# Weight conversion in three places of a step, one raw reload, eight transfers of v for a pair

## Chip, cores and metric

The kernel runs on one core of a Trainium2 chip. The metric is device time in microseconds (us), from the start to the end of one execution. Three runs of the kernel before took 1021.04, 1021.47 and 1020.66 us (median 1021.04).

## What is computed

Attention over the 256 channels of q, k and v (N = 6016 rows), and behind it two dense layers with a hidden width of 2048, all in float32:

```
qn = q / (norm(q, axis=rows) + 1e-6);  kn = k / (norm(k, axis=rows) + 1e-6)
s  = kn.T @ qn / tau;  s = s - s.max(-1);  a = exp(s);  a = a / (a.sum(-1) + 1e-9)
x  = v @ a                                        # 6016 x 256
x  = (h * sigmoid(1.702 * h)) @ w_out,   h = x @ w_in      # layer one
x  = max(0.01 * h, h) @ w2_out,          h = x @ w2_in     # layer two
```

The four weight matrices come as float64 numbers, seen by the kernel as pairs of 32-bit words.

## The kernel before

**Tiling.** The 6016 rows are cut into 6 pairs of two blocks of 512 rows (448 in the last pair). Each layer treats the pairs one after another: `steps` lists 12 of them, numbered i = 0 to 11, layer one being i = 0 to 5. Within a pair there are 8 steps f = 0 to 7; step f takes two blocks of 128 hidden units, f and f + 8. Every float32 operand is split into a high and a low part (`halves`, `subtract`), and every product is three matmuls (`terms`, L94).

**Four forms of a step.** Pair 0 is done plainly (`hidden_first`, L894), while the attention matrix is folded into `w_in` (`fold`, L685). Pairs 1 to 3 use `step` (L995): the hidden products come from seven block products on seven sums of weight blocks (A11, A12, A22, S1 to S4), the output products are plain: 45 matmuls a step. From pair 4 on (`FIRST`) `strassen_step` (L1082) does the output products in seven block products too: 39 matmuls a step, and weights are streamed from DRAM (`stream_in`, `stream_out`). The last two steps are plain again.

**Work on the weights.** For each f there are four pieces: `wi`, `wo` (layer one) and `w2i`, `w2o` (layer two). `convert` (L215) makes float32 of the two words: a scaling on ScalarE (`scale_words`, L192), three bit operations on VectorE (L225, L230, L234), then the high part as a cast and the low part as a subtraction. `combine` (L181) makes the sums of blocks with four additions of 128x128. The pieces of layer one are written raw to DRAM (`w1raw`, `o1raw`), and read back later one by one into `ts` (`load_first`, L311) for `combine_first` and `combine_out`, which also cast and subtract on VectorE. Results for streaming go to DRAM tiles `w1a`, `w1o`, `w2a`, `w2o`, with high parts first and low parts behind them.

**Order.** The whole order is written by hand: engines get their instructions in the order of the Python statements. The work on the weights is one generator (`jobs`, L348). `go_on(n)` takes n pieces from it, `to_mark` goes on to the next mark. In `step`, one `to_mark` stands ahead of the step's last output products (L1042) and one at its end (L1056); behind each stands `fetch` (one move of the next pair's input: a transpose from `xr` to `stg`, a subtraction, or a cast with a subtraction; `prefetch`, L785). In the next step VectorE then makes the low part of `gd` (`finish_step`, L1048, called by `next_stage` at L1013), and adds `tt` (L1020). TensorE's product S4 (L1033) writes to `pa`, which that addition reads, so it waits for it; after S4 VectorE adds `cc` (L1034). On ScalarE the copy to `tt` (L1016) is followed by the cast of `g11` (L1025), the activation of `tt`, the cast of `g22` (L1028) and the activations of `cc`.

**Buffers.** `xr` has two buffers of 512 columns, filled by four transfers each (`load`, L792), so 16 a pair. `cv` (raw words) has three, `ta` two and `ws` (cast parts) two buffers. All these transfers are issued by SP's queue.

Of the kernel before, what the change touches and what calls it, by code (L numbers as in the profile page):

```python
# [7 lines left out]
F32 = mybir.dt.float32  # L8
# [9 lines left out]
def tile_kernel(  # L18
# [31 lines left out]
    P = 128  # L50
# [69 lines left out]
    with tc.manual_schedule():  # L120
# [5 lines left out]
        def weights(pool, f):  # L126
            wa[f] = pool.tile([P, 2, 7, P], F32R, tag=f"wa{f}", name=f"wa{f}")
            wo[f] = pool.tile([P, 2, 2, C], F32R, tag=f"wo{f}", name=f"wo{f}")
# [48 lines left out]
        def next_load():  # L177
            if to_load and len(raws) < 3:
                load_piece(to_load.pop(0))

# [34 lines left out]
        def convert(key):  # L215


            name, f = key
            if key not in scaled:
                scale_words(raws[key])  # L220
                scaled.add(key)
# [17 lines left out]
            next_load()  # L239
            scale_next()  # L240
            yield
            a = a.bitcast(F32)
            flat = a.rearrange("p k c -> p (k c)")
            if name == "wo":
                hi, lo = (wo[f][:, s].rearrange("p k c -> p (k c)") for s in range(2))
                for j in range(2):
                    nc.sync.dma_start(
                        out=o1raw[f][:, 0::3] if j == 0 else o1raw[f][:, 1:3],
                        in_=a[:, 2 * j:2 * j + 2],
                    )  # L250
# [5 lines left out]
            if name == "wi":  # L256
# [14 lines left out]
            yield name == "w2i"  # L271
            if name == "w2o":
                if f >= REST:
                    nc.vector.tensor_copy(hi[:, 7], a[:, 3])
                    yield
                    subtract(lo[:, 7], a[:, 3], hi[:, 7].bitcast(F32))
                    yield
                raw = early.tile([P, P], F32, tag="wr", name="wr")
                nc.vector.tensor_copy(raw, a[:, 1])
                nc.sync.dma_start(out=w2r[:, f], in_=raw)  # L280
                yield True
            yield from combine(a)
            nc.vector.tensor_copy(hi[:, 3:7], a)
            yield
            def keep_block(x, n):
                if name == "w2i":
                    nc.sync.dma_start(out=w2a[f][:, n], in_=x[:, :7].bitcast(F32))
                elif f >= REST:
                    nc.sync.dma_start(out=w2o[f][:, n], in_=x.bitcast(F32))
                else:  # L290
                    for at in (slice(0, 3, 2), slice(3, 7)):
                        nc.sync.dma_start(out=w2o[f][:, n, at], in_=x[:, at].bitcast(F32))

            keep_block(hi, 0)
# [1164 lines left out]
```

## Time and profile before

| what | value |
|---|---|
| median of three runs | 1021.04 us |
| the profiled execution's own time | 1019.2 us |
| its span, first to last instruction | 1017.3 us |
| TensorE (PE) busy, share of the span | 1006.0 us, 99% |
| VectorE (DVE) busy | 894.2 us, 88% |
| ScalarE (ACT) busy | 727.8 us, 72% |
| chain that ended last | PE 88%, DVE 6%, DMA 3%, issue 2%, ACT 1% |

The profile is of one execution, and shorter than the median of the timed runs by 1.8 us. A busy PE is not a PE at its peak, since matmuls overlap and their ends are modelled: so the table does not tell how much time is lost in a stretch, and starts of matmuls have to be compared. The steps of pairs 1 to 3 lie between 147 and 397 us of the span, the first step with streamed weights begins at 396.73 us. The rows themselves stand two sections further down.

### The profile page before, as it was taken

To read this page: it belongs to the slowest core of one execution; us is meant where nothing else is said; L and a number is where in the kernel's file an instruction comes from. 1 tells how busy PE (TensorE), PEld (TensorE's weight loads), DVE (VectorE), ACT (ScalarE), POOL (GpSimd) and SP (SyncE) were. 2 spreads that over 40 slices of the span, in tenths; PEclk is the share of its full clock that TensorE was granted. 3 is DMA by queue.
4 is the path that set the end of the run, shared out by engine and by line. 5 is a ranking of instruction groups with operands and counts; after the bars stand their busy time and mean duration, and the time that the engine had idled before them with its cause. 6 is when DMAs were issued, how large, how long until landed. Compare 5 with 4: busy or idle time off the path is not lost.

```text
span 1017.3 us, 13086 instructions
## 1 busy us (share of the span) xinstructions
PE 1006.0 (99%) x4416; PEld 817.5 (80%) x4416; DVE 894.2 (88%) x1331; ACT 727.8 (72%) x1139; POOL 0.8 (0%) x7
## 2 busy tenths in 40 slices
PE   9999999999999999999999999999999999999998
PEld 7888877778788887787897887887887787787896
DVE  7899877888998998898998998998998998998985
ACT  7675456667677666787786886886887787687682
POOL 0000000000000000000000000000000000000000
PEclk9999999999999999999999999999999999999999
DMA  9866557655535854675766755865866765765662
GB/s 349 261 172 200 156 192 209 222 174 160 181 113 164 243 198 142 192 243 166 263 220 197 255 191 171 231 211 178 227 194 201 186 228 182 199 231 169 174 206 45
DMA packets 187186, 200.88 MB, mean 197 GB/s; under 512 B 102128, under 2 KB 144624, under 8 KB 185968
## 3 DMA queue, kind: packets, MB, share of 16 engines
q1 hardware_dynamic: 182832, 199.07, 62.9%
q10 hardware_dynamic: 4288, 0.98, 0.5%
q8 instruction: 35, 0.57, 0.2%
q14 instruction: 31, 0.25, 0.1%
HBM read 155.19 MB, written 44.83 MB: 197 GB/s over the span
## 4 chain that ended last, share of the span: by engine, by line
PE 88%; DVE 6%; DMA 3%; issue 2%; ACT 1%; SPq 1%; DVEq 0%; ACTq 0%
PE h L98 49%; PE y L98 16%; PE y L739 13%; PE y L1190 5%; PE y L465 4%; DMA qk<-in_k_dram 1%; DVE ta L234 1%; DVE ta L230 1%; DMA cv<-in_moe_w_in_dram 1%; DVE gd L105 1%; DMA ts<-w1raw 0%; DVE gd L102 0%; DVE ta L105 0%; DVE tt L105 0%; DVE ta L225 0%
## 5 line engine op out<-in xcount | busy, mean ns | idle before, releaser
L98 PE MATMUL h<-xa,wi 128*128 128x512 f32 (+1 forms) x765 | 200.9, 384 | 0.0
L98 PE MATMUL y<-g,wo 128*128 128x512 f32 (+1 forms) x744 | 198.4, 388 | 0.5 <-issue 0.5
L98 PEld LDWEIGHTS h<-xa,wi 128*128 128x128 f32 x765 | 142.9, 188 | 27.3 <-ACT tv L1098 1.4
L98 PEld LDWEIGHTS y<-g,wo 128*128 128x128 f32 x744 | 139.1, 188 | 29.7 <-issue 4.5
L98 PE MATMUL h<-xb,wi 128*128 128x512 f32 (+1 forms) x573 | 152.8, 391 | 0.1
L105 DVE TENSOR_TENSOR g<-t,g 128x1024 fp32r<-128x1024 f32 (+1 forms) x124 | 147.3, 1188 | 0.0
L739 PE MATMUL y<-gd,wo 128*128 128x512 f32 (+1 forms) x498 | 125.9, 390 | 4.1 <-DVE gd L102 2.2
L98 PEld LDWEIGHTS h<-xb,wi 128*128 128x128 f32 x573 | 106.9, 188 | 24.9 <-issue 3.6
L739 PEld LDWEIGHTS y<-gd,wo 128*128 128x128 f32 x498 | 93.0, 188 | 25.3 <-DVE gd L102 4.3
L98 PE MATMUL h<-xa,wa 128*128 128x512 f32 x384 | 104.2, 390 | 0.1
L98 PE MATMUL h<-g,wo 128*128 128x512 f32 (+1 forms) x372 | 102.6, 384 | 0.0
L709 ACT ACTIVATE g<-g 128x512 f32<-128x512 f32 (+1 forms) x92 | 57.8, 628 | 44.1 <-DVE g L105 42.8
L98 PE MATMUL h<-xb,wa 128*128 128x512 f32 x312 | 85.7, 397 | 0.6 <-DVE tt L105 0.2
L1138 ACT CAST g<-t 128x1024 fp32r<-128x1024 f32 (+1 forms) x62 | 63.9, 1031 | 28.6 <-DVE t L105 28.5
L98 PEld LDWEIGHTS h<-xa,wa 128*128 128x128 f32 x384 | 71.6, 188 | 15.2 <-DVE cc L105 0.5
L98 PEld LDWEIGHTS h<-g,wo 128*128 128x128 f32 x372 | 69.8, 188 | 12.5
L739 PE MATMUL y<-g,wo 128*128 128x512 f32 (+1 forms) x297 | 79.1, 388 | 0.0
L105 DVE TENSOR_TENSOR g<-g,g 128x1024 fp32r<-128x1024 f32 (+1 forms) x62 | 73.9, 1191 | 0.5
L105 DVE TENSOR_TENSOR t<-g 128x1024 f32<-128x1024 f32 (+1 forms) x62 | 73.5, 1186 | 0.0
L98 PEld LDWEIGHTS h<-xb,wa 128*128 128x128 f32 x312 | 57.2, 188 | 17.5 <-DVE tt L105 6.0
L1113 ACT CAST g<-g 128x1024 fp32r<-128x1024 f32 (+1 forms) x62 | 63.7, 1027 | 2.0
L739 PEld LDWEIGHTS y<-g,wo 128*128 128x128 f32 x297 | 55.8, 188 | 11.4
(177 smaller groups left out, 1449.0 us busy)
## 6 DMA issues: line engine op xcount, KB each, us to landing
wi<-w2a SPq DMA_DIRECT2D x48, 896.0 KB, 5.3
wo<-w2o SPq DMA_DIRECT2D x46, 640.0 KB, 4.8
wi<-w1a SPq DMA_DIRECT2D x16, 896.0 KB, 5.6
wo<-w1o SPq DMA_DIRECT2D x16, 640.0 KB, 5.2
cv<-in_moe_w_in_dram SPq DMA_DIRECT2D x32, 256.0 KB, 3.4
w1a<-wa SPq DMA_DIRECT2D x8, 896.0 KB, 4.6
wo<-w2o SPq DMA_DIRECT2D x48, 128.0 KB, 2.6
stg<-x SPq DMA_DIRECT2D x5, 1024.0 KB, 4.8
```

The lines of the kernel that those rows point to most:

```text
L98: nc.tensor.matmul(dst, lhsT=w, rhs=x, start=start, stop=stop, skip_group_check=more)
L105: nc.vector.tensor_tensor(out=out, in0=in0, in1=in1, op=op)
L230: nc.vector.scalar_tensor_tensor(out=a, in0=b, scalar=-0x80000000, in1=a, op0=ALU.bitwise_and, op1=ALU.bitwise_or)
L234: nc.vector.scalar_tensor_tensor(out=a, in0=b, scalar=3, in1=a, op0=ALU.logical_shift_left, op1=ALU.bitwise_or)
L465: nc.tensor.matmul(s_ps[h][:, :C], lhsT=t[:, 1, r, h * P:(h + 1) * P], rhs=t[:, 0, r, :], start=(j == 0 and r == 0), stop=(j == last and r ...
L709: nc.scalar.activation(out=out, in_=in_, func=AF.Prelu, alpha=0.01)
L739: nc.tensor.matmul(ys[key][kc], lhsT=ws[x], rhs=y, start=first and n == 0, stop=closing or (final and n == 2), skip_group_check=closing,)
L1113: nc.scalar.copy(g0[0], g[:, 0::2])
L1138: nc.scalar.copy(g1[0], t13)
L1190: nc.tensor.matmul(sums[i, M1], lhsT=kept_raw[layer][:, f], rhs=keep[i, f // 4][:, f % 4, :w], start=False, stop=True, skip_group_check=True,)
```

## The change

The sums of layer one now come for `wi` and `wo` of one f together. Both raw pieces lie in one DRAM tile `raw1[f]`, which `load_piece` reloads in one transfer into a buffer of `cv`, queued like the other loads behind the last piece of layer one, and not before the fold of that f (`folded`).

In `step` the work on the weights has three places in place of two marks. `run_casts` behind the copy to `tt` casts high parts (and scales the next piece's words) on ScalarE; `run_due` ahead of the last output products does the low parts, and the block sums of layer two; `begin_next` at the end of the step begins the next job (the eight additions of one f of layer one, or the bit operations of one piece of layer two). `close`, between the cast of `g22` and the product S4, makes the last low part of layer two's pieces. During pair 0 (`ahead`) the generator still does the sums one after another, with the casts on VectorE. Before pair 4 what is left is run at once.

High and low parts lie side by side in all weight tiles (`[P, 7, 2, P]` for `[P, 2, 7, P]`), and the blocks of the output weights are reordered so that a streamed step reads its six in one transfer. The index edits that follow from this are left out below. `v` comes in one buffer of 1024 columns, filled by four transfers and used twice a pair.

```
...
-    w1raw = [dram.tile([P, 4, P], F32, name=f"w1raw{f}") for f in range(NF)]
-    w2a = [dram.tile([P, 2, 7, P], F32, name=f"w2a{f}") for f in range(NF)]
-    w2o = [dram.tile([P, 2, 8, P], F32, name=f"w2o{f}") for f in range(NF)]
+    raw1 = [dram.tile([P, 2, 4, P], F32, name=f"raw1{f}") for f in range(NF)]
+    w2a = [dram.tile([P, 7, 2, P], F32, name=f"w2a{f}") for f in range(NF)]
+    w2o = [dram.tile([P, 8, 2, P], F32, name=f"w2o{f}") for f in range(NF)]
-    w1a = [dram.tile([P, 2, 7, P], F32, name=f"w1a{f}") for f in range(NF)]
-    w1o = [dram.tile([P, 2, 7, P], F32, name=f"w1o{f}") for f in range(NF)]
-    o1raw = [dram.tile([P, 4, P], F32, name=f"o1raw{f}") for f in range(NF)]
...
-        to_load, to_convert = list(order), list(order)
+        to_convert = list(order)
+        to_load = order[:2 * NF] + [("both", f) for f in range(NF)] + order[2 * NF:]
+        folded = set()
...
+            if name == "both":
+                t = raws[key] = early.tile([P, 2, 4, P], F32, tag="cv", name="cb", bufs=3)
+                nc.sync.dma_start(out=t, in_=raw1[f])
+                return
...
         def next_load():
-            if to_load and len(raws) < 3:
+            while to_load and len(raws) < 3:
+                if to_load[0][0] == "both" and to_load[0][1] not in folded:
+                    return
                 load_piece(to_load.pop(0))
+                if len(to_load) >= 4 * NF:
+                    return
...
-            hi, lo = (
-                early.tile([P, 8, P], F32R, tag="ws", name=f"{name}{x}", bufs=2) for x in "hl"
-            )
-            at = slice(0, 3, 2 if name == "w2o" and f < REST else 1)
-            nc.vector.tensor_copy(hi[:, at], a[:, at])
-            yield
-            subtract(lo[:, at], a[:, at], hi[:, at].bitcast(F32))
...
+        casts, due, closing = [], [], []
+        ahead = [True]
+        def new_blocks(name):
+            return early.tile([P, 4, 2, P], F32R, tag="ws", name=name, bufs=2)
+        def high(out, in_):
+            copy = nc.vector.tensor_copy if ahead else nc.scalar.copy
+            casts.append(lambda: copy(out(), in_))
+        def sums_first(f):
+            while ("both", f) not in raws:
+                next_load()
+            t = raws["both", f]
+            kept = {}
+            def out_blocks():
+                kept["x"] = new_blocks("wt")
+                return kept["x"][:, :, 0]
+            yield from combine(t[:, 0])
+            high(lambda: wa[f][:, 3:, 0], t[:, 0])
+            yield from combine(t[:, 1])
+            high(out_blocks, t[:, 1])
+            def second():
+                subtract(wa[f][:, 3:, 1], t[:, 0], wa[f][:, 3:, 0].bitcast(F32))
+                combined.add(f)
+                nc.sync.dma_start(out=w1a[f], in_=wa[f].bitcast(F32))
+                x = kept["x"]
+                subtract(x[:, :, 1], t[:, 1], x[:, :, 0].bitcast(F32))
+                nc.sync.dma_start(out=w1o[f][:, 2:6], in_=x.bitcast(F32))
+                for j in range(2):
+                    nc.sync.dma_start(
+                        out=w1o[f][:, j], in_=wo[f][:, :, j, j * P:(j + 1) * P].bitcast(F32)
+                    )
+                stored.add(("wo", f))
+                raws.pop(("both", f))
+                next_load()
+            due.append(second)
+        def words_of(key):
+            name, f = key
+            while key not in raws:
+                next_load()
+            if key not in scaled:
+                scale_words(raws[key])
+                scaled.add(key)
+            words = bits(key)
+            for _ in words:
+                pass
+            a = words_out.pop(key)
+            later = order.index(key) + 1
+            if later < len(order) and order[later] in raws:
+                nxt = order[later]
+                scaled.add(nxt)
+                casts.append(lambda: scale_words(raws[nxt]))
+            kept = {}
+            plain = name == "w2o" and f >= REST
+            some = slice(0, 3) if name == "w2i" else slice(0, 4) if plain else slice(0, 3, 2)
+            dst = (w2a if name == "w2i" else w2o)[f]
+            def base_blocks():
+                kept["x"] = new_blocks(name)
+                return kept["x"][:, some, 0]
+            def rest_blocks():
+                kept["y"] = new_blocks(name + "s")
+                return kept["y"][:, :, 0]
+            high(base_blocks, a[:, some])
+            def second():
+                x = kept["x"]
+                subtract(x[:, some, 1], a[:, some], x[:, some, 0].bitcast(F32))
                 if name == "w2i":
...
+                    nc.sync.dma_start(out=dst[:, :3], in_=x[:, :3].bitcast(F32))
                 else:
...
+                    nc.sync.dma_start(out=dst[:, :2], in_=x[:, 0::2].bitcast(F32))
+                    if plain:
+                        nc.sync.dma_start(out=dst[:, 6:], in_=x[:, 1::2].bitcast(F32))
+                    raw = early.tile([P, P], F32, tag="wr", name="wr")
+                    nc.vector.tensor_copy(raw, a[:, 1])
+                    nc.sync.dma_start(out=w2r[:, f], in_=raw)
+                for _ in combine(a):
+                    pass
+                casts.insert(0, lambda: nc.scalar.copy(rest_blocks(), a))
+                closing.append(third)
+            def third():
+                y = kept["y"]
+                subtract(y[:, :, 1], a, y[:, :, 0].bitcast(F32))
                 nc.sync.dma_start(
...
+                    out=dst[:, 3:7] if name == "w2i" else dst[:, 2:6], in_=y.bitcast(F32)
                 )
...
+                stored.add(key)
...
+            due.append(second)
+        def run_casts():
+            todo = list(casts)
+            casts.clear()
+            for item in todo:
+                item()
+        def run_due():
+            todo = list(due)
+            due.clear()
+            for item in todo:
+                item()
+        sums_left = list(range(NF))
+        words_left = order[2 * NF:]
+        def close():
+            while closing:
+                closing.pop(0)()
+        def begin_next():
+            if sums_left:
+                for _ in sums_first(sums_left.pop(0)):
+                    pass
+            elif words_left:
+                words_of(words_left.pop(0))
+        def tick():
+            run_casts()
+            close()
+            run_due()
+            begin_next()
 
         def jobs():
             for key in order[:2 * NF]:
                 yield from convert(key)
...
+            while ahead and sums_left:
+                yield from sums_first(sums_left.pop(0))
+                run_casts()
+                yield
+                due.pop()()
+                yield
...
+        def load_pair(p, kc):
+            w = width[p]
+            t = early.tile([P, 2 * BLK], F32, tag="xr", name="xr")
+            s = start_of(p, 0)
+            for a in range(P // SB):
+                cols = slice(kc * P + a * SB, kc * P + (a + 1) * SB)
+                nc.sync.dma_start(
+                    out=t[a * SB:(a + 1) * SB, :2 * w].rearrange("j (b i) -> j b i", i=SB),
+                    in_=v[s:s + 2 * w, cols].rearrange("(b j) i -> j b i", j=SB),
+                )
+            return t[:, :w], t[:, w:2 * w]
...
             load(0)
             yield
-            load(1)
+            yield
             yield
             place(0)
+            yield
+            place(1)
             load(2)
             yield
-            place(1)
-            load(3)
             yield
             t = staging(("x", layer, p))[:, :, :w]
             if layer == 2:
                 nc.sync.dma_start(out=t, in_=x2[p])
 
             place(2)
-            yield
             place(3)
             yield
...
+                t = ow[i, f] = slot(2 * k + 1, [P, 6, 2, P], f"wo{i}")
+                src = (w2o if i >= NPAIR else w1o)[f]
...
+                    nc.sync.dma_start(out=t.bitcast(F32), in_=src[:, :6])
...
             product(pb, S3, T3, more=True)
             nc.scalar.copy(tt, pb)
+            run_casts()
             between(i, f)
...
             beyond(i, f)
+            close()
             outputs(2)
...
-                if f or i == 2:
-                    to_mark()
+                run_due()
                 fetch()
...
-            if f < NF - 1:
-                to_mark()
+            if f < NF - 1 or i == 1:
+                begin_next()
             fetch()
...
-            ta, tb = (early.tile([P, BLK], F32, tag="xr", name=x, bufs=2)[:, :w] for x in "ab")
+            t = early.tile([P, 2 * BLK], F32, tag="xr", name="ab")
+            ta, tb = t[:, :w], t[:, BLK:BLK + w]
...
-            if i == FIRST:
+            fetch()
+            if i == 1:
+                ahead.clear()
                 for _ in work:
                     pass
+            if i == FIRST:
+                while words_left or casts or due or closing:
+                    tick()
             for f in range(NF):
                 while f not in combined:
...
```

## Rows read from the trace of the kernel before

**Rows 1.** Windows: window, length, each engine's busy us and instruction count, granted clock, DMA.
```profile
147.36:155.57 8.21, 7.95 (x35) 5.93 (x33) 5.55 (x10) 5.92 (x12) 0.00 (x0) 1.00 0.01 2
147.36:229.24 81.88, 80.86 (x350) 64.94 (x348) 67.59 (x134) 53.74 (x90) 0.00 (x0) 1.00 0.59 188
229.24:313.28 84.04, 83.27 (x362) 67.04 (x360) 75.12 (x143) 58.10 (x97) 0.00 (x0) 1.00 0.49 154
313.28:396.73 83.45, 83.19 (x361) 67.05 (x360) 73.86 (x140) 58.08 (x97) 0.00 (x0) 1.00 0.62 196
396.73:417.58 20.85, 19.47 (x82) 14.97 (x81) 17.44 (x29) 14.20 (x22) 0.00 (x0) 1.00 0.43 123
417.58:426.42 8.84, 8.84 (x40) 7.32 (x39) 8.48 (x11) 6.95 (x11) 0.00 (x0) 1.00 0.76 273
```

**Rows 2.** Timeline of 119 to 129 us: start, length, engine, line, tiles, idle before.
```profile
124.31 0.29 DVE L105 TENSOR_TENSOR ts<-ts 128x128 f32<-128x128 f32 x1 [4.23 <-DMA ts<-w1raw]
...
128.63 1.66 PE L739 MATMUL y<-gd,wo 128*128 128x512 f32 x6 [1.96 <-DVE gd L105]
```

**Rows 3.** Timeline of one step of pair 2, 276 to 289 us.
```profile
276.66 0.59 ACT L1016 COPY tt<-h 128x512 f32<-128x512 f32 x1 [0.76 <-PE h L98]
...
277.14 0.63 ACT L1025 CAST g<-tp 128x512 fp32r<-128x512 f32 x1
...
277.86 0.68 DVE L105 TENSOR_TENSOR tt<-tt,h 128x512 f32<-128x512 f32 x1
...
278.59 1.65 PE L98 MATMUL h<-xb,wa 128*128 128x512 f32 x6
...
279.59 0.69 DVE L105 TENSOR_TENSOR cc<-tv,h 128x512 f32<-128x512 f32 x1 [0.45 <-PE h L98]
...
280.20 0.69 DVE L105 TENSOR_TENSOR g<-tt,g 128x512 fp32r<-128x512 f32 x1
...
280.80 0.42 DVE L225 TENSOR_SCALAR ta<-cv 128x512 int32<-128x512 int32 x1
...
281.30 0.67 ACT L195 ACTIVATE cv<-cv 128x512 f32<-128x512 f32 x1
...
282.71 0.29 DVE L268 CAST w2oh<-ta 128x256 fp32r<-128x256 f32 x1
...
283.03 0.43 DVE L105 TENSOR_TENSOR w2ol<-ta,w2oh 128x256 fp32r<-128x256 f32 x1
...
283.51 0.69 DVE L102 TENSOR_TENSOR xa<-stg,xa 128x512 fp32r<-128x512 f32 x1
...
284.11 1.26 DVE L105 TENSOR_TENSOR ta<-ta 128x128 f32<-128x128 f32 x4
...
285.41 0.43 DVE L283 CAST w2oh<-ta 128x512 fp32r<-128x512 f32 x1
...
285.87 0.69 DVE L105 TENSOR_TENSOR w2ol<-ta,w2oh 128x512 fp32r<-128x512 f32 x1
...
286.48 0.68 DVE L105 TENSOR_TENSOR stg<-stg 128x512 f32<-128x512 f32 x1
...
287.08 1.22 DVE L102 TENSOR_TENSOR gd<-cc,gd 128x1024 fp32r<-128x1024 f32 x1
...
288.22 0.68 DVE L105 TENSOR_TENSOR tt<-tt,h 128x512 f32<-128x512 f32 x1
...
288.95 1.66 PE L98 MATMUL h<-xb,wa 128*128 128x512 f32 x6
```

**Rows 4.** Timeline: a longer stall in pair 2, and the second step of pair 4.
```profile
257.22 0.50 PE L739 MATMUL y<-gd,wo 128*128 128x512 f32 x1 [0.68 <-DVE gd L102]
...
409.08 1.63 PE L98 MATMUL y<-g,wo 128*128 128x512 f32 x6 [0.51 <-issue]
```

**Rows 5.** DMA issues: out, in, queue, count, size, median us from issue to landing.
```profile
w2a<-w2ih SPq DMA_DIRECT2D x8, 448.0 KB, 2.9
```

**Rows 6.** Waits of VectorE, 147 to 397 us: total, times, longest.
```profile
DVE w2il L105 <- DMA w2o<-w2ol: 0.9, 1, 0.9
```

More of the change, by code (lines that the diff above doesn't have):

```diff
@@ L213, in scale_next, with bits @@
                     return
[L215 to L221, printed above, removed]
+        words_out = {}
+        def bits(key):
             t = raws[key]
@@ L297, in convert @@
-            stored.add(key)
-            yield True
-        ready, combined, stored = {}, set(), set()
-        first_weights = {}
-        combine_order = [("wi", f) for f in range(3)]
-        for f in range(NF):
-            combine_order.append(("wo", f))
-            if f + 3 < NF:
-                combine_order.append(("wi", f + 3))
-        to_combine = list(combine_order)
-        def load_first():
-            if to_combine:
-                name, f = to_combine.pop(0)
-                a = early.tile([P, 4, P], F32, tag="ta", name="ts", bufs=2)
-                nc.sync.dma_start(out=a, in_=(w1raw if name == "wi" else o1raw)[f])
-                first_weights[name, f] = a
@@ L350, in jobs @@
                 yield from convert(key)
-            load_first()
-            for name, f in combine_order:
-                yield from (combine_first if name == "wi" else combine_out)(f)
-            for key in order[2 * NF:]:
-                yield from convert(key)
+            while ahead and sums_left:
[4 more added lines that the diff above has]
+                yield
         work = jobs()
@@ L361, in go_on @@
                 next(work, None)
-        def to_mark():
-            while not next(work, True):
-                pass
         big = [front.tile([P, 2, 2, 4, C], F32, name=f"qk{i}") for i in range(4)]
@@ L678, in tile_kernel @@
         fold_half(raw0, 0, 1)
-        nc.sync.dma_start(out=w1raw[0], in_=raw0)
+        nc.sync.dma_start(out=raw1[0][:, 0], in_=raw0)
+        folded.add(0)
         split_v(1, 1)
@@ L693, in fold @@
                 fold_scale(raw, pw[:, kc], kc)
-            hi, lo = wa[f][:, 0, :4], wa[f][:, 1, :4]
+            hi, lo = wa[f][:, :4, 0], wa[f][:, :4, 1]
             nc.vector.tensor_copy(hi, raw)
             subtract(lo, raw, hi.bitcast(F32))
-            nc.sync.dma_start(out=w1raw[f], in_=raw)
+            nc.sync.dma_start(out=raw1[f][:, 0], in_=raw)
+            folded.add(f)
         fctx.close()
@@ L733, in put @@
             if closing:
-                ws = tuple(ow[LAST, g][:, x, 3 if kc > s else kc + s] for x in range(2))
+                ws = tuple(ow[LAST, g][:, ((0, 3), (2, 1))[s][kc], x] for x in range(2))
             else:
@@ L788, in prefetch @@
             x = xa[p % 2 if layer == 1 else (NPAIR + p) % 2]
-            at = [(kc, u) for kc in range(KC) for u in range(2)]
             blocks = {}
             def load(i):
-                if layer == 1:
-                    kc, u = at[i]
-                    blocks[i] = early.tile([P, BLK], F32, tag="xr", name="xr", bufs=2)
-                    for a in range(P // SB):
-                        nc.sync.dma_start(
-                            out=blocks_in(blocks[i], p, a), in_=blocks_of(v, p, u, kc, a)
-                        )
+                if layer == 1 and i % 2 == 0:
+                    blocks[i], blocks[i + 1] = load_pair(p, i // 2)
             def place(i):
@@ L803, in place @@
                     nc.vector.transpose(
-                        out=staging(("x", layer, p))[:, i, :w], in_=blocks.pop(i)[:, :w]
+                        out=staging(("x", layer, p))[:, i, :w], in_=blocks.pop(i)
                     )
@@ L821, in prefetch @@
             place(2)
-            yield
             place(3)
@@ L1079, in out_product @@
             t = ow[i, f]
-            terms(sums[i, m], (t[:, 0, block], t[:, 1, block]), xs, f == 0, f == split_steps(i) - 1)
+            terms(sums[i, m], (t[:, block, 0], t[:, block, 1]), xs, f == 0, f == split_steps(i) - 1)
         def strassen_step(i, f):
@@ L1261, in load_v @@
         def load_v(p, n):
-            b = vblocks_in[n] = early.tile([P, BLK], F32, tag="xr", name="xr", bufs=2)
-            for a in range(P // SB):
-                nc.sync.dma_start(out=blocks_in(b, p, a), in_=blocks_of(v, p, n % 2, n // 2, a))
+            if n % 2 == 0:
+                vblocks_in[n], vblocks_in[n + 1] = load_pair(p, n // 2)
         def place_v(i, n):
-            nc.vector.transpose(out=staged_x[i][:, n], in_=vblocks_in.pop(n)[:, :width[i % NPAIR]])
+            nc.vector.transpose(out=staged_x[i][:, n], in_=vblocks_in.pop(n))
         def cast(to, i, n, j):
```

101 lines of the change are left out of this document (29 added, 72 removed).

## The prediction

> **What bounds the kernel.** I read the table of engines first (PE busy for 99% of the span), then asked in windows how much of that is real. In a step behind pair 4 TensorE does 39 matmuls in 8.84 us (last row of [rows 1]; the matmuls are counted by their weight loads, the number in brackets under PEld), so 0.2267 us for each, without a wait. Take that as the price, and the steps of layer one show what "busy" hides. Pair 1: 348 matmuls are 78.88 us, the window is 81.88: 3.00 us lost. Pair 2: 360 are 81.60 of 84.04: 2.44 lost. Pair 3: 81.60 of 83.45: 1.85. The first two steps of pair 4: 81 are 18.36 of 20.85: 2.49. With the one stall of 1.96 us in pair 0 [rows 2] that is 11.7 us, and it is all that this change can reach: it alters nothing of what TensorE computes, and behind 418 us nothing of what it waits for.
>
> Who takes those 11.7 us is seen next, in the timeline of one ordinary step [rows 3]. S4 begins at 278.59, the next S4 at 288.95: 10.36 us for 45 matmuls that need 10.20. Each S4 begins 0.05 us behind the end of VectorE's addition `tt` (277.86 and 0.68). Follow VectorE from there: it idles once, 0.45 us ahead of `cc`, which waits for S4, and then works without a gap through 280.20, 280.80, and so on to the next `tt` at 288.22. So S4 waits for `tt`, `cc` for S4, and `tt` for everything on VectorE between: a closed loop of 10.36 us. In these steps VectorE is the bound, not TensorE. Longer stalls are the same queue running later: at 257.22 TensorE waits 0.68 us for the low part of `gd` [rows 4], which stands between the conversion and `tt`.
>
> **The change, part by part.** *The reload.* In pair 0 VectorE stands still for 4.23 us for a raw block that was asked for only when it was needed, and TensorE pays 1.96 us a little later [rows 2]. After the change the reloads are queued with the other loads, as soon as a buffer of raw words is free, which for the first ones is some 8 us earlier by the order of the code. The wait goes. The generator's pieces get somewhat heavier (ten pieces hold 8 additions, 2 casts, 2 subtractions, against six for 4, 1 and 1), which the 4.23 us cover. Gain 1.9 us, bounds 1.0 and 1.96.
>
> *Fewer operations on VectorE, in other places.* I work it out for the step of [rows 3]. What VectorE now does between two `tt` takes, from start to start: `g11`, `cc` and `g22` some 0.60 each (279.59 to 280.20, 280.20 to 280.80), bit operations 1.91 (280.80 to 282.71), the cast 0.32, its subtraction and the raw copy 0.48, `fetch` 0.60, additions 1.30 (284.11 to 285.41), cast 0.46, subtraction 0.61, `fetch` 0.60, `gd` 1.14, `tt` 0.68. The change takes the two casts away (0.78) and moves the 0.61 of the last subtraction to `close`, into the place where VectorE idled.
>
> But it adds a wait. On ScalarE three operations now stand behind the copy to `tt`: two high parts and the scaling. Behind them are queued the cast of `g11`, the activation of `tt`, the cast of `g22`; behind `g11`'s cast waits VectorE's subtraction for it, and behind that all of VectorE, `cc` and so TensorE's next write to `pa`. The sum, in that step's clock: ScalarE's next start is 277.14. The cast of 128x512 is 0.63 (the row of 277.14 is one of the same shape). The cast of 128x256 or 128x384 is not in the trace on ScalarE: above 0.31 (half of that) and below 0.63, I take 0.50, nearer to the whole since instructions have a fixed part (on VectorE half the columns cost 0.29 against 0.43). Scaling 0.67. So `g11`'s cast starts at 278.94 and ends at 279.57, where it ended at 277.77. VectorE from there: `g11` 0.60, `close` 0.60, `cc` 0.61, `g22` 0.60 (its cast ends at 280.83, early enough): 281.98. `run_due`: 0.48 and 1.30: 283.76. `fetch` 0.60: 284.36. Bit operations 1.91: 286.27. `fetch` 0.60, `gd` 1.14: 288.01. `tt` 0.68 and 0.05: 288.74. TensorE's own time for that S4 is 278.59 + 45 x 0.2267 = 288.79. So the loop opens, with 0.05 us to spare, against 0.16 us late before; the bounds of the unknown cast move it by 0.2 us either way. In the steps that prepare layer one's sums it is much easier: two low parts of 0.60 and eight additions of 2.6, no scaling, no `close`.
>
> The low part of `gd`, ahead of `tt`, is early by the same sum: the places where a whole mark of 2.4 to 2.9 us and a transpose stood ahead of it are the longer stalls, and they go. By pair: pair 1 loses 0.73 in its first step of 33 matmuls (first row of [rows 1]), where the generator has no work and VectorE is busy for 5.55 of 8.21 us, so that stays; of the other 2.27 I take back 2.0. Pair 2: 2.0 of 2.44. Pair 3: 1.4 of 1.85. In pair 4's first step VectorE still had a piece of layer two to finish; by the count of jobs it no longer does. (Pair 0 calls 109 pieces, 80 of them for the conversions; 29 are nearly three sums of ten. That leaves 5 sums and 16 pieces, 21 jobs, for 8 + 7 + 7 = 22 places.) The 0.51 us at 409.08 [rows 4] are a wait for output banks, and stay with what belongs to it: 1.3 of 2.49. Together with the reload 8.6 us.
>
> From that I take 1.1 us for some 16 full steps in which 0.05 us of room is less than I know: two transposes now fall in one place in one step of a pair, and each unknown cast can be longer. Forecast: 7.5 us less.
>
> *Edits at nothing.* `v` in 8 transfers, and a streamed step's output weights in one: SP issues less, TensorE waited for neither, and the loads have one to two steps of cover; if the cover went, a late transpose would hold `gd` as at 257.22, 0.7 us a pair. The new layout leaves each operand's runs at 128 elements, and a cast to blocks two apart costs VectorE 0.29 for 256 columns, no more than its share [rows 3].
>
> A rule speaks against the move. The Trainium skill, ScalarE: Activation LUTs, section Rules for kernel authors, gives plain elementwise work to VectorE and not to ScalarE. The rows agree on the price: 0.63 us on ScalarE for 0.43 on VectorE [rows 3]. If ScalarE's time were what counts, 21 jobs with two casts of 0.20 more would cost 8.4 us, and the sum would be about nothing gained. I don't follow it here, since ScalarE is busy for 58.10 of 84.04 us in pair 2 [rows 1], 7.3 us a step, and gets 1.1 more; the row that would prove it right is VectorE waiting for a cast on ScalarE.
>
> **Rivals.** *ScalarE is passed on (0.20).* The chain above has no room; if casts come 0.3 us later or longer, S4 is late by about 0.3 in some 16 steps, 4.8 us of the 8.6 come back, and the gain is 3.8: 1017.2 us. For it: the 0.05. Against: the figures are full lengths, and ScalarE's operations overlap a little.
>
> *Only the reload counts (0.10).* The waits for `gd` and `tt` change names but not size; 1.0 to 1.9 us remain: 1019.5 us. Against it: 0.78 us less on VectorE in a loop without gaps. Also the case that the jobs don't finish in time and pair 4 starts as late as now comes near this side.
>
> *Slower: a cast waits for a store (0.08).* Place: `run_casts`, the cast into a buffer of `ws`, of which there are two. The buffer's last content is sent to DRAM by `run_due` of the step before, issued at about 282.5 in the clock above; with 2.9 us to land [rows 5] it is free at 285.4, and the cast wants it at 277.14 + 10.20 + 0.63 = 287.97. Cover 2.6 us. VectorE did once wait 0.9 us for such a store [rows 6]. If stores land later than 5.5 us behind their issue, every microsecond more is a microsecond for ScalarE, VectorE and S4. At 1.2 us over in 16 steps: 19.2 - 8.6 = 10.6 slower, 1031.6 us. It decides from about 0.55 us a step.
>
> *All of it goes (0.07).* The 1.1 us of doubt aren't needed, and half of the 0.73 and of the waits in pair 4 go too: 9.6 us, 1011.4.
>
> **How the numbers follow.** The forecast has 0.55, with a range of its own from 1012 to 1016. The sum is of the profiled execution (1019.2 us, its span 1017.3 and 1.9 around it): 1011.7 there. The median of the timed runs lies 1.84 higher, and I take the same difference from it: 1021.04 - 7.5 = 1013.5. The range for 8 in 10 takes in the case above, and the ones below down to the reload alone: 1011 to 1019.5. A difference under 0.2% (2.0 us) can't be told from none here. Faster by more than that: 0.55 + 0.20 + 0.07 = 0.82. Within: 0.10. Slower: 0.08.
>
> **What would show it.** Right: no wait for `ts` at 120 us; steps of pairs 2 and 3 at 10.20 us from S4 to S4; VectorE idle some 1 us a step, ended by ScalarE's cast of `g11`; no piece of layer two behind 397 us. Wrong: S4 or the third matmul of `gd` still waiting for VectorE in most steps; ScalarE ahead of its first cast held by a DMA; SP's queue with a load of raw words late; anything above 8.84 us a step behind 418 us.

## The result, and the profile after

The changed kernel took 1010.77 us (median of 4 runs, 1010.57 to 1011.19), the kernel before 1021.25 us beside it (4 runs, 1020.66 to 1021.56): ratio 0.9899, 95% interval 0.9881 to 0.9916. That is 10.5 us less where 7.5 were forecast, and 0.23 us below the low end of the range. The profiled execution of after took 1010.57 us, its span is 1008.8.

Windows of after, cut as in [rows 1]: the first step of pair 1, pairs 1, 2 and 3, then the first two and the third step of pair 4.

```profile
144.57:152.78 8.21, 7.96 (x34) 5.93 (x32) 6.66 (x12) 5.92 (x12) 0.00 (x0) 1.00 0.55 204
144.57:224.32 79.75, 79.49 (x349) 65.18 (x348) 63.13 (x122) 60.04 (x104) 0.00 (x0) 1.00 0.62 209
224.32:306.75 82.43, 81.92 (x361) 67.44 (x360) 71.03 (x134) 64.72 (x114) 0.00 (x0) 1.00 0.50 163
306.75:388.73 81.98, 81.98 (x362) 67.36 (x360) 66.18 (x122) 63.06 (x109) 0.00 (x0) 1.00 0.61 193
388.73:408.00 19.27, 18.83 (x83) 15.05 (x82) 13.18 (x17) 14.17 (x22) 0.00 (x0) 1.00 0.30 74
408.00:416.84 8.84, 8.84 (x41) 7.32 (x40) 8.50 (x11) 6.94 (x11) 0.00 (x0) 1.00 0.99 329
```

Against [rows 1] each window is shorter by 0.00 (first step, as forecast), 2.13, 1.61, 1.47 and 1.58 us, and pair 1 starts 2.79 us earlier; some 0.5 us of that is there at 53 us already, far ahead of any reload. Together 9.58 us by the third step of pair 4. Behind that point the span is 1.1 us longer than before (1008.8 - 408.0 against 1017.3 - 417.58), of which the last section tells.

The reload in pair 0, in the timeline of after: the first two blocks are asked for from 108.27 on, 11.6 us earlier than the first block of before (119.83), the first has landed by 111.5, and VectorE's first sum of the reloaded blocks at 119.12 has nothing to wait for ([rows 2] had 4.23 us there, and TensorE's 1.96).

```profile
108.27 3.48 SPq L152 DMA_DIRECT2D cb<-raw  x2
...
119.12 0.28 DVE L104 TENSOR_TENSOR cb<-cb 128x128 f32<-128x128 f32 x1
```

One full step of pair 2 in the timeline of after, which answers to [rows 3] (L1084 copies to `tt`, L371 and L290 are high parts, L204 scales, L1094 and L1097 cast `g11` and `g22`):

```profile
281.11 0.59 ACT L1084 COPY tt<-h 128x512 f32<-128x512 f32 x1 [0.76 <-PE h L97]
...
281.60 0.63 ACT L371 CAST w2is<-ta 128x512 fp32r<-128x512 f32 x1
281.86 0.69 DVE L104 TENSOR_TENSOR tt<-tt,h 128x512 f32<-128x512 f32 x1
...
282.12 0.66 ACT L204 ACTIVATE cv<-cv 128x512 f32<-128x512 f32 x1
...
282.68 0.40 ACT L290 CAST w2o<-ta 128x256 fp32r<-128x256 f32 x1
...
282.95 1.52 PE L97 MATMUL h<-xb,wa 128*128 128x512 f32 x6
282.97 0.62 ACT L1094 CAST g<-tp 128x512 fp32r<-128x512 f32 x1
...
283.62 0.69 DVE L104 TENSOR_TENSOR g<-tp,g 128x512 fp32r<-128x512 f32 x1 [1.07 <-ACT g L1094]
```

`tt` ends at 282.55 and S4 starts at 282.95, without a wait: 0.40 us of room. VectorE idles 1.07 us, ended by ScalarE's cast of `g11`, the wait that the prediction named. The waits of VectorE from 144 to 389 us, then of TensorE from 50 to 420 us, in after (total, times, longest):

```profile
DVE g L104 <- ACT g L1094: 21.1, 23, 1.8
DVE tt L104 <- PE h L97: 16.6, 17, 1.9
```

```profile
PE h L97 <- DVE xb L101: 0.5, 1, 0.5
PE y L97 <- issue: 0.4, 1, 0.4
PE h L97 <- DVE tt L104: 0.2, 1, 0.2
```

The order has turned: VectorE waits for TensorE 17 times at `tt`. In before there were 5 such waits. TensorE waits for VectorE twice in all; in before it waits 5 times for `gd` (4.2 us together) and once for `tt`. That S4 was late by some 0.16 us a step in before is hardly seen in this view, but in the distance from the end of `tt` to S4. In before it is 0.05 or 0.06 us in 17 of the 24 steps of pairs 1 to 3, in after in two (the first step of pair 1, and one behind a stall at 344.46), and about 0.40 in the others. Two losses are new, in the timeline of after. At 228.19 TensorE waits for the split of `xb`, ahead of which the last `begin_next` of pair 1 now stands. At 344.46 ScalarE's cast waits 0.46 us for the store of a `ws` buffer: the price of the slower rival, paid once.

```profile
228.19 0.50 PE L97 MATMUL h<-xb,wa 128*128 128x512 f32 x1 [0.51 <-DVE xb L101]
...
344.46 0.51 ACT L290 CAST w2i<-ta 128x384 fp32r<-128x384 f32 x1 [0.46 <-DMA w2o<-w2o]
```

### The profile page after: what moved, and what is told of

Its sections match the earlier page's. It is cut to its first block, busy times and chain, and to the rows that moved or that the text cites. A ratio compares the mean times of both kernels' runs of the same rounds, so it can differ in the third digit from the quotient of the medians.

```text
span 1008.8 us, 12925 instructions
## 1 busy us (share of the span) xinstructions
PE 1002.4 (99%) x4416; PEld 819.9 (81%) x4416; DVE 874.7 (87%) x1285; ACT 746.0 (74%) x1181; POOL 0.8 (0%) x7
## 4 chain that ended last, share of the span: by engine, by line
PE 98%; DVE 1%; issue 0%; DMA 0%; ACT 0%; DVEq 0%
PE h L97 53%; PE y L806 17%; PE y L97 17%; PE y L1260 5%; PE y L530 4%; PE h L677 1%; PE h L567 0%; DMA cv<-in_moe_w_in_dram 0%; PE h L806 0%; DVE cc L104 0%; DVE ta L104 0%; PE y L677 0%; DVE ta L236 0%; DVE g L104 0%; PE y L635 0%
## 5 line engine op out<-in xcount | busy, mean ns | idle before, releaser
L97 PEld LDWEIGHTS y<-g,wo 128*128 128x128 f32 x744 | 139.1, 188 | 30.0 <-issue 4.4
L104 DVE TENSOR_TENSOR g<-tt,h 128x512 f32<-128x512 f32 (+1 forms) x62 | 41.5, 670 | 28.5 <-ACT tt L1175 20.8
```

The lines of the kernel that those rows point to most:

```text
L97: nc.tensor.matmul(dst, lhsT=w, rhs=x, start=start, stop=stop, skip_group_check=more)
L104: nc.vector.tensor_tensor(out=out, in0=in0, in1=in1, op=op)
```

## The experiments

Each ratio is to runs of the kernel before on the same chip. The theory at the start was the prediction's: two casts less on VectorE and a subtraction in its idle time open the loop. The rivals were that one of the two suffices, that the reload carries most of it, and that the spreading of the work over the step does it.

**The kernel before once more.** Nothing is edited.

> The kernel before, unchanged. Its profiled execution took 1019.2 us where its timed runs take 1021.25, and the changed kernel's took 1010.6 where its timed runs take 1010.8. Theory (pace): the steps of 448 rows (pairs 5 and 11) have two paces, 7.90 and 8.06 us a step, whatever the kernel; the profiled execution of before had the quick one in all ten such steps, most executions have the slow one. Then this profile shows 8.06 us in most of them and takes 1020.5 to 1021.5 us. Rival (waits): the 2 us are lost in pairs 0 to 4, to waits that differ from run to run; then the steps of pairs 5 and 11 take 7.90 us again and the windows of pairs 0 to 4 are 1 to 2 us longer than 147.4 + 249.4 us.

1019.58 us, ratio 0.9999 (0.9989 to 1.0009). The noise leaves 1 us open in such a comparison. Its profiled execution took 1018.87 and has the quick pace of the last section again, with no loss in pairs 0 to 4 that would bear out the rival, so it doesn't decide between the two.

**The casts back on VectorE, at their new places.**

```diff
-            copy = nc.vector.tensor_copy if ahead else nc.scalar.copy
+            copy = nc.vector.tensor_copy
...
-                casts.insert(0, lambda: nc.scalar.copy(rest_blocks(), a))
+                casts.insert(0, lambda: nc.vector.tensor_copy(rest_blocks(), a))
```

> The changed kernel with every cast back on VectorE, at the same place of its program order; the three places, the reload and the layout stay. Theory (places): what opened the loop is that the last subtraction moved into the time in which VectorE waited for S4, and that the work is spread; casts on VectorE cost 0.78 us a full step, of which the 0.4 us of room and the 0.9 us that VectorE now waits for ScalarE's cast of g11 take all: 1010 to 1012 us, no wait of VectorE for that cast. Rival (engine): the move to ScalarE is what counts; then S4 is late by 0.2 to 0.3 us in some 16 full steps again: 1014 to 1016 us.

1010.58 us, 0.9916 (0.9901 to 0.9930), not told apart from after. So the move to ScalarE is not what opened the loop. One step of 11.79 us is left, where VectorE's cast waits for a store, in the timeline:

```profile
343.11 0.43 DVE L371 CAST w2os<-ta 128x512 fp32r<-128x512 f32 x1 [1.13 <-DMA w2a<-w2is]
```

**`close` moved back**, just ahead of `run_due`.

```diff
             beyond(i, f)
-            close()
             outputs(2)
...
             if layer == 1:
+                close()
                 run_due()
```

> The changed kernel with the last low part (close) just ahead of run_due, behind g22's subtraction, in place of ahead of S4's addition. Theory (chain): the 0.6 us then stand in VectorE's chain from g11's cast to tt, which has some 0.4 us of room in a full step; S4 is late by 0.1 to 0.2 us in some 16 steps: 1012.5 to 1014 us. Rival (sum): VectorE has 1 to 1.5 us idle a step, so that its place does not matter: 1010.8 us.

1010.27 us, 0.9913 (0.9899 to 0.9928). The gain doesn't hang on that place either.

**Both undone at once**: casts on VectorE and `close` late, both edits above. This asks whether either of the two suffices, or neither is needed.

> The changed kernel with both undone: every cast on VectorE, and close just ahead of run_due. Each alone cost nothing (1010.6 and 1010.3 us). Theory (either suffices): VectorE's closed loop from S4 to S4 was 0.16 to 0.2 us too long; 0.78 us of casts taken from it, or 0.6 us of subtraction moved out of it, opens it; with neither it is as long as before, full steps take 10.35 to 10.45 us again, S4 waits for tt: 1012.5 to 1014 us. Rival (spread): the loop was too long only because two marks of unequal size stood in it; one job a step, begun at the end of a step, is enough, full steps stay at 10.20 us: 1010 to 1011 us.

1009.59 us, 0.9895 (0.9881 to 0.9910). The theory that either of the two suffices falls with this run: neither is needed. The same kinds of operation as before, on the same engine, now let S4 come every 10.20 us in most steps (pair 3 has some of up to 10.39). One step in its timeline, from `cc` to `cc`:

```profile
274.08 0.69 DVE L104 TENSOR_TENSOR cc<-tv,h 128x512 f32<-128x512 f32 x1 [0.33 <-PE h L97]
...
276.47 1.27 DVE L104 TENSOR_TENSOR ta<-ta 128x128 f32<-128x128 f32 x4
277.66 0.69 DVE L101 TENSOR_TENSOR xa<-stg,xa 128x512 fp32r<-128x512 f32 x1
...
279.44 0.69 DVE L240 SCALAR_TENSOR_TENSOR ta<-cv,ta 128x512 int32<-128x512 int32 x1
280.05 0.68 DVE L104 TENSOR_TENSOR stg<-stg 128x512 f32<-128x512 f32 x1
...
281.79 0.42 DVE L371 CAST w2is<-ta 128x512 fp32r<-128x512 f32 x1
282.12 0.29 DVE L290 CAST w2o<-ta 128x256 fp32r<-128x256 f32 x1
282.33 0.68 DVE L104 TENSOR_TENSOR tt<-tt,h 128x512 f32<-128x512 f32 x1
...
284.28 0.69 DVE L104 TENSOR_TENSOR cc<-tv,h 128x512 f32<-128x512 f32 x1 [0.33 <-PE h L97]
```

Look at who stands behind whom. The cast at 281.79 is followed after 0.33 us by an operation that doesn't need it, 0.09 ahead of its end. In [rows 3] the same cast (285.41) is followed by its own subtraction, after 0.46 us: 0.03 behind its end. The cast of 128x256: 0.21 here, 0.32 there. The additions: 1.19 here (276.47 to 277.66), 1.30 there. The third bit operation: 0.61 here; in before the cast of its result came 0.73 later (281.98 to 282.71). Its row in the timeline of before:

```profile
281.98 0.69 DVE L234 SCALAR_TENSOR_TENSOR ta<-cv,ta 128x512 int32<-128x512 int32 x1
```

Four such pairs stood in each full step and are parted now: 0.13 + 0.11 + 0.11 + 0.12 = 0.47 us, and 10.36 - 0.47 = 9.89, an estimate, is below TensorE's 10.20. The step shown agrees: from `cc` to `tt` it takes 8.25 us (274.08 to 282.33) against 8.63 in [rows 3] (279.59 to 288.22). That is 0.38 less, though a subtraction of 128x384 in it takes the place of one of 128x256 and the raw copy, 0.10 more.

**The pairs put together again**, with one job a step kept: casts on VectorE and `close` late as in the run before, and each cast right ahead of its subtraction, behind the operations that make its input.

```diff
-            high(base_blocks, a[:, some])
+            nc.vector.tensor_copy(base_blocks(), a[:, some])
...
-                casts.insert(0, lambda: nc.scalar.copy(rest_blocks(), a))
-                closing.append(third)
+                nc.vector.tensor_copy(rest_blocks(), a)
+                third()
...
+            first()
             due.append(second)
```

> The changed kernel with every cast on VectorE, each directly ahead of the subtraction that needs it, and the operations of a piece of layer two in the order of before: bit operations, cast, subtraction and raw copy at the end of a step, additions, cast and subtraction ahead of the next step's last output products; close does nothing. The same instructions, with casts a step later and close just ahead of run_due, took 1009.6 us with full steps at 10.20. Theory (neighbours): on VectorE an instruction that needs its predecessor's result starts some 0.03 us behind its end, one that does not starts some 0.09 us ahead of it; the new places part four such pairs in a full step, 0.45 us, and this is what opened the loop of 10.36 us. Then full steps take 10.35 to 10.45 us again, 1011.5 to 1014 us. Rival (balance): the order within a job is of no account; 1009.5 to 1010.5 us.

1015.10 us, 0.9961 (0.9946 to 0.9975). In pair 2 the full steps are 10.36 us again, and every second one 10.6 (pair 3 has three steps of 10.20 and five of 10.35 to 10.80); pair 1, whose sums keep their places, stays at 10.20 but for its edges. Its timeline:

```profile
275.44 1.66 PE L97 MATMUL h<-xb,wa 128*128 128x512 f32 x6
...
278.94 0.43 DVE L373 CAST w2is<-ta 128x512 fp32r<-128x512 f32 x1
279.40 0.69 DVE L104 TENSOR_TENSOR w2is<-ta,w2is 128x512 fp32r<-128x512 f32 x1
...
282.52 0.29 DVE L355 CAST w2o<-ta 128x256 fp32r<-128x256 f32 x1
...
282.85 0.43 DVE L104 TENSOR_TENSOR w2o<-ta,w2o 128x256 fp32r<-128x256 f32 x1
...
285.07 0.68 DVE L104 TENSOR_TENSOR tt<-tt,h 128x512 f32<-128x512 f32 x1
...
285.80 1.43 PE L97 MATMUL h<-xb,wa 128*128 128x512 f32 x5
```

The distances are back (0.46 and 0.33), S4 starts 0.05 us behind `tt` again, and S4 to S4 is 10.36. So the neighbours are shown, from both sides, for pairs 2 and 3. Two other things are in the time. The steps of 10.6 have a cast of 128x384, which takes VectorE 0.55 us in the new layout (at 271.90) and took 0.36 in before (at 293.07). And the first step of pair 2 takes 11.91 us for 11.03 in after, since more of the first job now stands ahead of the splits of `xb`.

**The kernel before with layer two's casts on ScalarE, at the old places.**

```diff
-            nc.vector.tensor_copy(hi[:, at], a[:, at])
+            nc.scalar.copy(hi[:, at], a[:, at])
...
-            nc.vector.tensor_copy(hi[:, 3:7], a)
+            nc.scalar.copy(hi[:, 3:7], a)
```

> The kernel before with the high parts of layer two's pieces cast on ScalarE, at their old places in the program. Theory (places): VectorE's next instruction is the subtraction that needs the cast, so VectorE waits for ScalarE's queue and gains nothing by the move; a cast takes 0.4 to 0.6 us there and stands behind what ScalarE has to do: pairs 2 and 3 take 1 to 6 us longer, 1020 to 1026 us. Rival (engine): 0.8 us less of VectorE's work a step opens the loop here too: 1015 to 1017 us.

1076.27 us, 1.0545 (1.0525 to 1.0566): slower, by some ten times the most that was expected. A step of pair 2 in its timeline:

```profile
250.48 0.62 ACT L283 CAST w2oh<-ta 128x512 fp32r<-128x512 f32 x1 [2.51 <-DVE ta L105]
251.01 0.58 ACT L1003 COPY h<-h 128x512 f32<-128x512 f32 x1
251.13 0.69 DVE L105 TENSOR_TENSOR w2ol<-ta,w2oh 128x512 fp32r<-128x512 f32 x1 [0.68 <-ACT w2oh L283]
...
251.64 0.97 PE L98 MATMUL h<-xa,wa 128*128 128x512 f32 x3 [2.65 <-ACT h L1003]
```

ScalarE's queue stands 2.51 us for VectorE's additions, and behind that cast is the copy to `pb` for which TensorE waits 2.65. The place makes the price: a whole step in between costs nothing. The Trainium skill, ScalarE: Activation LUTs, Rules for kernel authors, gives plain elementwise operations such as `add` and `mul` to VectorE, and does not list casts. Carried over to casts it is neither borne out nor refuted by after: at the new places the two engines came to the same time.

**The reload asked for late.** First at the end of the job before, then one job ahead.

```diff
+        wanted = set()
...
-                if to_load[0][0] == "both" and to_load[0][1] not in folded:
+                if to_load[0][0] == "both" and to_load[0][1] not in (folded & wanted):
...
+            wanted.update((f, f + 1))
             while ("both", f) not in raws:
                 next_load()
+            next_load()        # second kernel only
```

> The changed kernel with a raw block of layer one asked for no earlier than one job ahead, as before; the first at the time it is needed. Theory: VectorE waits some 4 us for it near 120 us, TensorE 2 us, and nothing later: 1012.5 to 1013.2 us. Rival (cover): the rest of the change gives VectorE enough room by then, and no time is lost: 1010.8 us.

> The changed kernel with a raw block asked for exactly one job ahead (at the beginning of the job before it), the first one when it is needed. Asked for at the end of the job before it, it cost 38 us, VectorE waiting some 8 us for each. Theory: now only the first wait of some 4 us near 120 us is left, TensorE loses 1.8 to 2.2 us there: 1012 to 1013 us. Rival (cover): VectorE catches up by the time that TensorE needs it: 1010.5 us.

The first asks later than was meant, right where the next job begins: 1048.86 us, 1.0291 (1.0276 to 1.0307). VectorE waits seven times, up to 8.1 us (first row), and four steps of pair 1 take about 17 us. The second is what was meant: 1011.34 us, 0.9909 (0.9894 to 0.9924). VectorE waits twice, 3.8 us in all (second fence), TensorE 0.6 us once. Against after that is 0.6 us by medians, inside the noise; in the traces pair 1 starts 1.5 us later (146.09), 0.6 of it there at 53 us already, so that 0.9 are left. It is a lower bound for the reload: this version still asks for the first block at 117.97, which before did at 119.83. A block that is asked for one job ahead costs this little here; asked for right ahead of its job it costs 38 us.

```profile
DVE cb L104 <- DMA cb<-raw: 41.0, 7, 8.1
```

```profile
DVE cb L104 <- DMA cb<-raw: 3.8, 2, 2.8
...
PE y L809 <- DVE gd L104: 0.6, 1, 0.6
```

**`v` in 16 transfers** into the same wide buffer.

```diff
-                nc.sync.dma_start(
-                    out=t[a * SB:(a + 1) * SB, :2 * w].rearrange("j (b i) -> j b i", i=SB),
...
+                for u in range(2):
+                    nc.sync.dma_start(
+                        out=t[a * SB:(a + 1) * SB, u * w:(u + 1) * w].rearrange("j (b i) -> j b i", i=SB),
...
```

> The changed kernel with v in 16 transfers a pair, into the same wide buffer. Theory: no one waits for them, 1010.3 to 1011 us. Rival: SP's queue issues eight more, at some 0.5 us each, between the loads and stores of the weights, and a store of ws or a reload comes later: VectorE or ScalarE waits for a DMA in some steps, 1011.5 to 1013 us.

1012.04 us, 0.9930 (0.9916 to 0.9945); the interval only touches that of after. A store lands late, a cast waits 1.61 us for it, and two steps of pair 3 take 11.24 and 10.65 us. With 8 transfers such a wait is there at nearly the same place, 0.46 us in after and 1.13 in the run with the casts on VectorE; so that the 16 made it longer is likely, and not shown. In its timeline:

```profile
345.28 0.62 ACT L371 CAST w2os<-ta 128x512 fp32r<-128x512 f32 x1 [1.61 <-DMA w2a<-w2is]
```

**The new stall removed**: `close` late, and the last `begin_next` of pair 1 behind the splits for pair 2.

```diff
-            if f < NF - 1 or i == 1:
+            if f < NF - 1:
                 begin_next()
...
                 switch(*steps[i + 1])
+                if i == 1:
+                    begin_next()
```

> The changed kernel with close just ahead of run_due, and the job that was begun at the end of pair 1 begun behind the three splits of the next pair's second input in place of ahead of them. TensorE waited for those splits (0.51 us, 0.83 us lost in the first step of pair 2). Theory: that loss goes, all else stays: first step of pair 2 at 10.20 to 10.35 us, 1009.4 to 1009.9 us. Rival: the 1.9 us of bit operations only come to stand ahead of gd's low part and tt in that step, and cost there what they cost before: 1010.3 us.

1008.77 us (1008.56 to 1009.94), 0.9889 (0.9873 to 0.9906). TensorE's waits over the same stretch have lost the row of `xb`, and the first step of pair 2 takes 10.33 us for 11.03. It is the quickest version by its median; its interval overlaps that of after.

```profile
PE y L97 <- issue: 0.4, 1, 0.4
PE h L97 <- DVE tt L104: 0.2, 1, 0.2
```

**The same, and the first two output products of pair 4 exchanged**, against the wait of 0.4 us that stays in both.

```diff
-                slots.extend([one(M3, 3, g0, 1), one(M1, 0, g0, 0)])
+                two = [one(M3, 3, g0, 1), one(M1, 0, g0, 0)]
+                slots.extend(two[::-1] if (i, f) == (FIRST, 0) else two)
```

> The kernel of close_late_switch_first (1008.8 us), with the first two output products of pair 4 exchanged: the first then writes the bank that VectorE copies first. TensorE waits there 0.44 us, 0.9 us lost in that step. Theory: 0.5 to 0.7 us less in that step, 1008.1 to 1008.3 us. Rival: the second product then waits for the second copy as long as the first does now; 1008.8 us.

1009.24 us (1008.40 to 1009.98), 0.9905 (0.9889 to 0.9922). The step is 0.55 us shorter in the trace; the timed runs can't tell it.

**The kernel before, profiled a third time**, for the difference between its profiled execution and its median.

> The kernel before, unchanged, one look. In two profiled executions of it (1019.2 and 1018.9 us) all steps of 448 rows had the quick pace of 7.90 us; other kernels showed the slow pace of 8.06 us in pair 5, pair 11 or both, 0.16 us a step and up to 1.6 us in all. Theory: executions of it that take 1020.5 us or more have the slow pace in pair 5 or 11; if this one takes 1020.5 or more, its profile shows it, and if it takes 1019.5 or less it does not. Rival: a slow execution with the quick pace in both, the time lost elsewhere.

1020.94 us, one execution. Its windows of 119 to 140 us, TensorE behind the stall, and the same matmuls in the execution of before that was profiled first:

```profile
119.00:130.00 11.00, 9.09 (x45) 7.45 (x44) 6.54 (x17) 3.36 (x5) 0.00 (x0) 0.98 0.60 187
130.00:140.00 10.00, 10.00 (x40) 8.13 (x39) 8.79 (x19) 4.47 (x8) 0.00 (x0) 0.86 0.80 272
```

```profile
128.18 3.56 PE L739 MATMUL y<-gd,wo 128*128 128x512 f32 x10 [1.91 <-DVE gd L105]
```

```profile
128.63 2.56 PE L739 MATMUL y<-gd,wo 128*128 128x512 f32 x10 [1.96 <-DVE gd L105]
```

After the stall the granted clock of 130 to 140 us is 0.86, a mix of its two levels of 1.2 and 2.4 GHz, and ten matmuls take 3.56 us, where the ten behind the stall of [rows 2] took 2.56 in all. Pair 1 starts at 148.50, 1.14 us later than in the execution profiled first, which had the same stall and kept 1.00. Another 0.6 us are lost by the end, where pair 11 has the slow pace of the last section. Together that is the 1.7 us between 1019.2 and 1020.94. The theory is met in part: the slow pace is there, but the greater part of the loss lies elsewhere, as the rival had it.

## Why the prediction came out as it did

**The place and the mechanism of the loss: right.** The 11.7 us were where the prediction put them, and the loop over VectorE was what made a step 10.36 us. Of the 23 steps of 45 matmuls all but three (10.34, 11.03 and 10.54 us) lie within 0.03 of 10.20, layer two's pieces end inside pair 3, VectorE waits for the cast of `g11` about 0.9 us a step, and behind 408 us a step takes 8.84.

**The terms.** Reload 1.9: pair 1 starts 2.79 us earlier, 2.3 of it behind 53 us (not all of it need be the reload's). Pairs: 2.0, 2.0, 1.4, 1.3 forecast, 2.13, 1.61, 1.47, 1.58 measured. Sum 8.6 against 9.1 without the 0.5 ahead of 53 us. Pair 2 lacks its 0.4 since the stall for `xb` was not foreseen: the prediction did not list what the `begin_next` at the end of pair 1 stands ahead of, the splits that pair 2 starts with.

**First step that failed: the 1.1 us taken off for doubt**, because the chain had only 0.05 us to spare, with another 0.05 counted between the end of `tt` and S4. It had 0.35 by the same count, 0.40 between the two in the trace. The chain put ScalarE's operations end to end: 2.28 us from the copy's start to `g11`'s cast with those lengths (the small cast at 0.50), against 1.86 in the trace (281.11 to 282.97), since each starts about 0.1 us ahead of the other's end and the small cast takes 0.40. The rival "ScalarE is passed on" noted that overlap and did not put a number on it; in [rows 3] it can be read (277.14 begins 0.11 us ahead of the end of 276.66). In the profiled execution the forecast was 1011.7, and 1010.57 came: the miss is that 1.1. That it fits so closely is luck: 9.1 us for 8.6 within the sum's reach, and 0.5 more ahead of 53 us, made good the 1.1 lost behind 408 us.

**Second step that failed: the offset of 1.84 us, carried from before to after.** The median of before lies 2.05 us above its profiled execution, that of after 0.20 above its own. The offset was no constant of timing, and not even one of the kernel: in the first experiment the kernel before has 0.71 (1019.58 against 1018.87). In the third profile it was a falling clock behind the stall, and pace; after has no such stall. The recorded mean clock of each execution shows how often it fell. Of 38 executions of before that have one, 13 stand at 0.997 or 0.998, and these took 1020.01 to 1021.89 us; of the 25 at 0.999 or 1.00, 23 took 1018.09 to 1019.89. Of the 36 executions of after and of the eight versions of it that came out between 1008 and 1016 us, none stands below 0.999. So part of the gain by medians is likely that this fall is gone. Where in an execution the clock fell is shown in the one profile alone, and the four runs of before that stand beside after have no clock on record.

**Right in sum, wrong in reason.** The prediction gave the opened loop to 0.78 us of casts less on VectorE and 0.61 in `close`. Undoing both costs nothing. What opens it in pairs 2 and 3 is that dependent neighbours on VectorE are parted (0.47 us a step, of which the prediction's own list held the signs: 0.46 and 1.30 between starts for lengths of 0.43 and 1.26). Putting the pairs together again costs 4.3 us by medians (1015.10 against 1010.77), and 5.5 against the 1009.59 of the version from which it differs by that order alone; some 1 us of this is the longer stall for `xb`. That pair 1's gain comes from one job a step in place of marks of uneven weight was not tried by itself. Of the reload's term 0.6 to 0.9 us are shown by themselves; how much more of the 2.3 us in pair 0 is the reload's stays open.

**Edits at nothing.** The 8 transfers of `v` are worth some 1.3 us, by medians whose intervals touch; what 16 cost is not the transposes, as the prediction had it, but a `ws` store landing late. So the slower rival's mechanism is real: 0.46 us once in after, 1.13 and 1.61 in two experiments. It never met 16 steps. The layout is not free either: 0.29 for 256 columns is more than half of 0.43, and a cast of 128x384 on VectorE went from 0.36 to 0.55 us. In after that cast stands on ScalarE.

## What to carry to other kernels

In a loop that one engine closes, list the distances between starts, not the lengths: an operation right behind the one whose result it needs shows its own small gap, and independent work put between them takes the gap away without removing anything. An operation given to another engine must find its operand ready there, or all that is queued behind it waits. Compare medians with medians: the offset between one profiled execution and the timed runs is no constant to carry over, and may be part of what the change removes.

## What had not been expected of the hardware

The steps of 448 rows (pairs 5 and 11) have two paces, at one granted clock: two steps of pair 5 in after, a window each,

```profile
484.47:492.37 7.90, 7.90 (x40) 7.33 (x39) 6.50 (x9) 6.85 (x12) 0.00 (x0) 1.00 0.99 402
508.37:516.43 8.06, 8.06 (x40) 7.32 (x39) 7.70 (x11) 6.96 (x12) 0.00 (x0) 1.00 0.60 213
```

39 matmuls in 7.90 or 8.06 us, without a wait. The pace holds over a stretch of steps and can change within a pair (here at 500 us). Before's first profile has the quick one in both pairs, after the slow one from there and in pair 11: that is the 1.1 us which the span behind 408 us is longer. Both paces came in several kernels; what sets it stays open.
